# Attention and feed-forward in one kernel: query and key loads in 2.3 KB runs, keys in even/odd order, a reordered opening, and attention steps taken further ahead

## The chip, the cores and the metric

One core of a Trainium2 chip. The time is the device time of one execution in microseconds (us), as the median of several executions. The spread of one kernel's runs is under 1.5%. A ratio is the mean time of one kernel's runs over that of the kernel before's runs on the same chip in the same rounds, so it is not quite the ratio of the medians quoted beside it. A bracket is its 95% interval.

## The reference, cut to what matters

```python
# 8 batches, 8 heads, 576 tokens, head size 64; window of 32 keys on each side
scores = scale * np.matmul(q, k.transpose(0, 1, 3, 2))       # scale = 1/8
scores = np.where(np.abs(pos[:, None] - pos[None, :]) <= 32, scores, -1e9)
attn = softmax(scores);  x = (attn @ v) as 4608 tokens x 512
h = x @ w_in                                                  # 512 -> 2048
out = np.maximum(0.01 * h, h) @ w_out                         # 2048 -> 512
```

q, k and v are drawn with a standard deviation of 0.1. A score is then a sum of 64 products of about 0.01 in size, scaled by 1/8: about 0.01. Every exponential is near 1, and the attention is nearly the plain mean of the values in the window.

## The kernel before

A step of attention handles two heads ("pair") and half a batch's tokens: five score products, one exponential on ScalarE, one mask product on GpSimd, ten products for the sums `s` and the values `x`, and a reciprocal and a product on VectorE. The feed-forward tiles (`h_tile`, `o_tile`) take the result `xT` in groups of 512 tokens. q and k are loaded in blocks of 64 tokens, cast, transposed on TensorE, and copied out of PSUM into `qT` and into `kbd`, where two heads stand on the block diagonal.

```python
# loads: one packet is one token's 64 numbers (256 bytes)
nc.sync.dma_start(
    out=t[64 * s:64 * s + 64, ab].rearrange("p u c d -> p (u c) d"),
    in_=src[b, h0:h0 + 2].rearrange("u (c p) d -> p (u c) d", p=64))
# ... [cut]
def cast_v(b, u):                       # two plain casts of 64x576
    nc.gpsimd.tensor_copy(out=vbd[b % 2][0:64, u, :, 0:64], in_=vf[0:64, u])
    nc.gpsimd.tensor_copy(out=vbd[b % 2][64:128, u, :, 64:128], in_=vf[64:128, u])
# ... [cut] copies of the transposes, each writes runs of 64 elements
nc.scalar.activation(
    out=qT[b][:, :, u, 64 * c0:64 * c1].rearrange("p s (c i) -> p c s i", i=64),
    in_=tp[:, 0:n], func=AF.Copy)
for r, eng in ((0, nc.scalar), (64, nc.vector)):
    dst = kt[r:r + 64, u:NPAIR:2, c0:c1, r:r + 64].rearrange("p s c i -> p c s i")
    # ... [cut] one half copied by ScalarE, the other by VectorE
# ... [cut] the main loop: tiles of a group, with the next group's steps spread behind them
for ci, (kind, a, m) in enumerate(chunks):
    want = start + -(-(goal - start) * (ci + 1) // len(chunks))
    todo = want - state["done"]
    # ... [cut] emit the h_tiles or the o_tile of this chunk
    for _ in range(todo):
        step()
```

The softmax here doesn't subtract the row's maximum and nothing guards it: scores larger than these inputs give would overflow.

Of the kernel before, what the change touches and what calls it, by code (L numbers as in the profile page):

```python
# [16 lines left out]
def kernel(  # L17
# [15 lines left out]
    W = 32  # L33
# [8 lines left out]
    FFC = DFF // 128  # L42

# [15 lines left out]
    def load_qk(src, b, name):  # L59

        t = fload.tile([128, 2, 2, NB, D], FP32, name=name)
        for s in range(2):
            for ab in range(2):
                h0 = 4 * ab + 2 * s
                nc.sync.dma_start(  # L65
                    out=t[64 * s:64 * s + 64, ab].rearrange("p u c d -> p (u c) d"),
                    in_=src[b, h0:h0 + 2].rearrange("u (c p) d -> p (u c) d", p=64),
                )
        return t

    def load_v(b):

        t = fload.tile([128, NPAIR, NB, D], FP32, name="vf")
        for ab in range(2):
            nc.sync.dma_start(
                out=t[64 * ab:64 * ab + 64].rearrange("p u c d -> p (u c) d"),
                in_=v[b, 4 * ab:4 * ab + 4].rearrange("u (c p) d -> p (u c) d", p=64),
            )
        return t

    loaded = {}

    def load_qks(b):
        if b < B:
            loaded[b] = [load_qk(q, b, "qf"), load_qk(k, b, "kf"), None]

    def load_vs(b):
        if b < B:
            loaded[b][2] = load_v(b)

    load_qks(0)
    load_vs(0)


# [4 lines left out]

    ones_bd = const.tile([128, 128], BF16)  # L100
    nc.vector.memset(ones_bd, 0.0)
    nc.vector.memset(ones_bd[0:64, 0:64], 1.0)
    nc.vector.memset(ones_bd[64:128, 64:128], 1.0)

    kbd = [const.tile([128, NPAIR, NB, 128], BF16, name=f"kbd{i}") for i in range(2)]
    vbd = [const.tile([128, NPAIR, NB, 128], BF16, name=f"vbd{i}") for i in range(2)]
    nc.vector.memset(kbd[0], 0.0)
    nc.vector.memset(vbd[0], 0.0)
# [3 lines left out]
        [(0, 0, 128), (1, 32, 128), (2, 96, 128), (3, 160, 128), (4, 224, 64)],  # L112
        [(5, 288, 128), (6, 352, 128), (7, 416, 128), (8, 448, 128), (4, 288, 64)],
    ]
    mask = [const.tile([128, 576], BF16, name=f"mask{i}") for i in range(2)]
    for hf in range(2):
        nc.gpsimd.memset(mask[hf], 1.0)
        for lo in (0, 64):
            c0 = 0
            for blk, q0, n in WIN[hf]:  # L120
                m = mask[hf][lo:lo + 64, c0:c0 + n]

                off = q0 - 64 * blk
                nc.gpsimd.affine_select(  # L124
                    out=m, in_=m, compare_op=ALU.is_ge, fill=0.0,
                    base=off + W, channel_multiplier=-1, pattern=[[1, n]],
                )
                nc.gpsimd.affine_select(  # L128
                    out=m, in_=m, compare_op=ALU.is_ge, fill=0.0,
                    base=W - off, channel_multiplier=1, pattern=[[-1, n]],  # L130
                )
                c0 += n
# [5 lines left out]

    qb, kb, qT = {}, {}, {}

    def cast_qk(b, u):
        if b >= B:
            return
        for i, name, into in ((0, "qb", qb), (1, "kb", kb)):
            if u == 0:
                into[b] = cast.tile([128, NB, 2, 2, D], BF16, name=name)
            nc.gpsimd.tensor_copy(  # L147
                out=into[b][:, :, u], in_=loaded[b][i][:, :, u].rearrange("p a c d -> p c a d"),
            )

    def cast_v(b, u):
        if b >= B:
            return
        vf = loaded[b][2]
        nc.gpsimd.tensor_copy(out=vbd[b % 2][0:64, u, :, 0:64], in_=vf[0:64, u])
        nc.gpsimd.tensor_copy(out=vbd[b % 2][64:128, u, :, 64:128], in_=vf[64:128, u])

    def transposes(b):

        qT[b] = attn.tile([128, 2, 2, S], BF16, name="qT")  # L160
        kt = kbd[b % 2]
        for u in range(2):
            for c0, c1 in ((0, 5), (5, 9)):
                for which, src in (("q", qb[b]), ("k", kb[b])):
                    n = c1 - c0
                    tp = tps.tile([128, 5, 2, 64], BF16, name="tp")
# [6 lines left out]
                    if which == "q":  # L173
                        nc.scalar.activation(  # L174
                            out=qT[b][:, :, u, 64 * c0:64 * c1].rearrange(
                                "p s (c i) -> p c s i", i=64),
                            in_=tp[:, 0:n], func=AF.Copy,
                        )
                    else:
                        for r, eng in ((0, nc.scalar), (64, nc.vector)):  # L180

                            dst = kt[r:r + 64, u:NPAIR:2, c0:c1, r:r + 64].rearrange(
                                "p s c i -> p c s i")
                            if eng is nc.scalar:
                                nc.scalar.activation(out=dst, in_=tp[r:r + 64, 0:n], func=AF.Copy)  # L185
                            else:
                                nc.vector.tensor_copy(out=dst, in_=tp[r:r + 64, 0:n])  # L187
# [3 lines left out]

    def score(i):
        b, hf, p = i // 8, (i // 4) % 2, i % 4
        ps = scps.tile([128, 1024], FP32, name="ps")
        c0 = 0
        for blk, q0, n in WIN[hf]:
            nc.tensor.matmul(  # L197
                ps[:, c0:c0 + n], kbd[b % 2][:, p, blk, :],
                qT[b][:, p // 2, p % 2, q0:q0 + n], start=True, stop=True,
            )  # L200
            c0 += n
        e = attn.tile([128, 576], BF16, name="e")
        nc.scalar.activation(out=e, in_=ps[:, 0:576], func=AF.Exp, scale=scale)  # L203
        pr = attn.tile([128, 576], BF16, name="pr")
        nc.gpsimd.tensor_mul(pr, e, mask[hf])  # L205
        probs[i] = pr

    def weighted(i):
        b, hf, p = i // 8, (i // 4) % 2, i % 4
# [3 lines left out]
        for dst, w in ((s, None), (x, vbd[b % 2])):  # L213
            c0 = 0
            for n_, (blk, q0, n) in enumerate(WIN[hf]):
                a = q0 - HALF * hf
                nc.tensor.matmul(  # L217
                    dst[:, a:a + n], ones_bd if w is None else w[:, p, blk, :],
                    pr[:, c0:c0 + n], start=(n_ == 0), stop=(n_ == len(WIN[hf]) - 1),
                    skip_group_check=True,  # L220
                )
                c0 += n
# [8 lines left out]
    def h_tile(g, t0, n, f):  # L231
        if f == 0:
            gT[g] = moe.tile([128, FFC, 512], BF16, name="gT")
        h = mmps.tile([128, 512], FP32, name="mm")
# [5 lines left out]
        nc.scalar.activation(out=gT[g][:, f, 0:n], in_=h[:, 0:n], func=AF.Prelu, alpha=0.01)  # L240

    def o_tile(g, t0, j):
        o = mmps.tile([128, 512], FP32, name="mm")
        for f in range(FFC):
            nc.tensor.matmul(  # L245
                o, gT[g][:, f, ts(j, 128)], w_out_bf[:, f, :],
# [7 lines left out]
    NC = 2 * NPAIR * B  # L254
    t_parts = {}
    state = {"tp": 0, "done": 0}
# [9 lines left out]
    def step():  # L266
# [4 lines left out]
        step_transposes(8 * (b + 1) + -(-r * 8 // 7))  # L271
        if i + 1 < NC:
            score(i + 1)
        weighted(i)
        if r in (0, 1):
            cast_qk(b + 1, r)
        if r == 2:
            load_qks(b + 2)
        if 2 <= r < 6:
            cast_v(b + 1, r - 2)  # L280
        if r == 6:
            load_vs(b + 2)
        state["done"] += 1

    cast_qk(0, 0)
    cast_qk(0, 1)
    w_in_r = moe_w_in.rearrange("(a u d) f -> a d u f", a=2, d=D)
    for u in range(DMC):
        for a in range(2):
            nc.gpsimd.dma_start(out=w_in_bf[64 * a:64 * a + 64, u, :], in_=w_in_r[a, :, u, :])  # L290
    for u in range(NPAIR):
        cast_v(0, u)
    load_qks(1)
    load_vs(1)
    nc.vector.memset(kbd[1], 0.0)
    nc.vector.memset(vbd[1], 0.0)
    w_out_r = moe_w_out.rearrange("(c p) f -> p c f", p=128)
    for c in range(0, FFC, 4):
        nc.gpsimd.dma_start(out=w_out_bf[:, c:c + 4, :], in_=w_out_r[:, c:c + 4, :])

    step_transposes(8)
    score(0)

    groups = [(0, 256)] + [(256 + 512 * i, 512) for i in range(8)] + [(256 + 512 * 8, 256)]
    need = [4 * -(-(t0 + n) // HALF) for t0, n in groups]
    for _ in range(need[0]):
        step()

    for g, (t0, n) in enumerate(groups):
        goal = need[g + 1] if g + 1 < len(groups) else NC  # L310
        chunks = []
        per = 4 if n == 512 else 8
        for f in range(0, FFC, per):
            chunks.append(("h", f, per))
        for j in range(n // 128):
            chunks.append(("o", j, 1))
        start = state["done"]
        for ci, (kind, a, m) in enumerate(chunks):
            want = start + -(-(goal - start) * (ci + 1) // len(chunks))
            todo = want - state["done"]  # L320
            if kind == "h":
                for f in range(a, a + m):
                    h_tile(g, t0, n, f)
            else:
                o_tile(g, t0, a)
            for _ in range(todo):
                step()
        while state["done"] < goal:
            step()

# [29 lines left out]
```

## Time and profile before

| | before |
|---|---|
| time | 422.3 us (421.9 to 422.55, 3 runs) |
| TensorE busy | 80% of the span |
| first w_in product | 63.9 us |
| waits of w_in products for `xT` | 17.2 us in 8 waits |
| copies out of PSUM, 640 columns | 0.50 to 0.70 us each |

The columns are line, engine, operation, output and input with partitions x elements, count; then busy us in all, mean ns of one; then idle time before it and what ended it. From the kernel before, groups by shape:

```profile
L155 POOL CAST vbd<-vf 64x576 bf16<-64x576 f32 x32 | 21.1, 659 | 0.1
L174 ACT ACTIVATE qT<-tp 128x640 bf16<-128x640 bf16 x16 | 11.2, 701 | 53.4 <-PE tp L168 53.4
L185 ACT ACTIVATE kbd<-tp 64x640 bf16<-64x640 bf16 x16 | 11.1, 695 | 22.1 <-PE tp L168 22.1
```

### The profile page before, as it was taken

The numbers are of one execution on the slowest core, as the hardware profiler recorded it, in microseconds if no ns is written. First come the engines' busy times: TensorE is split into PE (matmuls) and PEld (weight loads), VectorE is DVE, ScalarE is ACT, GpSimd is POOL, SyncE is SP. The second block draws the span as 40 slices with busy tenths as digits, with TensorE's granted clock in tenths as the row PEclk, the third lists the DMA queues.
The fourth block names the chain that finished last, engine by engine and source line by source line (L and its number), as shares of the span: only waits on it lengthen the run. The fifth ranks groups of instructions, "written<-read, shape, count | busy, mean of one in ns | idle before, by whom it ended". The sixth has DMA issues, their size and how long they took to land.

```text
span 421.2 us, 6100 instructions
## 1 busy us (share of the span) xinstructions
PE 338.7 (80%) x2464; PEld 194.5 (46%) x2464; DVE 202.3 (48%) x204; ACT 164.5 (39%) x289; POOL 176.5 (42%) x220
## 2 busy tenths in 40 slices
PE   0231058766999799979999997999899799989996
PEld 0120046643555365545555554565455445534472
DVE  6112043866466457634445765568357735740111
ACT  1140033622752274237237525732473255116050
POOL 8992153746426443633216553654355413200000
PEclk9999999989999899989999999999899989989999
DMA  9999999445871937192450956396301100110111
GB/s 163 207 202 198 190 136 193 77 69 122 130 114 61 205 60 138 61 199 43 92 121 4 197 136 102 65 188 128 60 0 46 55 2 2 51 50 2 50 51 50
DMA packets 119835, 42.33 MB, mean 100 GB/s; under 512 B 112640, under 2 KB 114688, under 8 KB 119808
## 3 DMA queue, kind: packets, MB, share of 16 engines
q1 hardware_dynamic: 117056, 37.76, 50.7%
q0 software_dynamic: 2752, 4.20, 5.5%
q8 instruction: 19, 0.31, 0.3%
q14 instruction: 8, 0.07, 0.1%
HBM read 36.70 MB, written 9.44 MB: 110 GB/s over the span
## 4 chain that ended last, share of the span: by engine, by line
PE 73%; POOL 9%; DVE 7%; SPq 3%; issue 3%; ACT 3%; DMA 2%; POOLq 0%; DVEq 0%
PE mm L236 31%; PE mm L245 29%; DVE r L224 5%; PE s L217 3%; SPq L65 3%; PE tp L168 3%; PE x L217 3%; PE ps L197 3%; DMA kf<-in_k_dram 2%; POOL pr L205 2%; POOL mask L128 1%; POOL mask L124 1%; DVE xT L226 1%; ACT qT L174 1%; POOL w_in_bf L290 1%
## 5 line engine op out<-in xcount | busy, mean ns | idle before, releaser
L236 PE MATMUL mm<-xT,w_in_bf 128*128 128x512 bf16 (+1 forms) x640 | 142.3, 380 | 17.2 <-DVE xT L226 17.2
L224 DVE RECIPROCAL r<-s 128x288 f32<-128x288 f32 x64 | 125.2, 1957 | 58.0 <-PE s L217 56.6
L205 POOL TENSOR_TENSOR pr<-e,mask 128x576 bf16<-128x576 bf16 x64 | 81.4, 1272 | 169.2 <-ACT e L203 168.8
L245 PE MATMUL mm<-w_out_bf,gT 128*128 128x512 bf16 x576 | 130.7, 382 | 0.0
L240 ACT ACTIVATE gT<-mm 128x512 bf16<-128x512 f32 (+1 forms) x160 | 88.7, 554 | 94.0 <-PE mm L236 92.7
L236 PEld LDWEIGHTS <-w_in_bf 128*128 128x128 bf16 x640 | 64.0, 103 | 81.8 <-issue 30.0
L245 PEld LDWEIGHTS <-gT 128*128 128x128 bf16 x576 | 54.8, 99 | 62.1 <-issue 1.7
L250 DVE COPY o_sb<-mm 128x512 f32<-128x512 f32 x36 | 24.9, 691 | 70.8 <-PE mm L245 70.8
L174 ACT ACTIVATE qT<-tp 128x640 bf16<-128x640 bf16 (+1 forms) x32 | 20.7, 648 | 80.4 <-PE tp L168 80.4
L187 DVE COPY kbd<-tp 64x640 bf16<-64x640 bf16 (+1 forms) x32 | 14.8, 461 | 76.8 <-ACT kbd L185 76.7
L203 ACT ACTIVATE e<-ps 128x576 bf16<-128x576 f32 x64 | 41.2, 643 | 22.5 <-PE ps L197 22.4
L168 PE MATMUL tp<-ident,qb 128*128 128x128 bf16 x144 | 14.7, 235 | 35.7 <-POOL qb L147 31.9
L185 ACT ACTIVATE kbd<-tp 64x640 bf16<-64x640 bf16 (+1 forms) x32 | 20.5, 641 | 48.5 <-PE tp L168 48.5
L217 PE MATMUL s<-pr,ones_bd 128*128 128x128 bf16 (+1 forms) x320 | 27.7, 220 | 8.3 <-POOL pr L205 7.4
L226 DVE TENSOR_TENSOR xT<-x,r 128x288 bf16<-128x288 f32 x64 | 29.3, 458 | 6.7
L168 PEld LDWEIGHTS <-qb 128*128 128x128 bf16 x144 | 11.5, 105 | 42.0 <-POOL qb L147 32.3
L197 PE MATMUL ps<-qT,kbd 128*128 128x128 bf16 (+1 forms) x320 | 27.9, 220 | 1.2 <-ACT e L203 1.1
L217 PE MATMUL x<-pr,vbd 128*128 128x128 bf16 (+1 forms) x320 | 27.9, 220 | 0.1
L168 PE MATMUL tp<-ident,kb 128*128 128x128 bf16 x144 | 14.6, 234 | 16.0 <-ACT qT L174 8.3
L197 PEld LDWEIGHTS <-kbd 128*128 128x128 bf16 x320 | 22.6, 102 | 5.1 <-issue 2.3
L217 PEld LDWEIGHTS <-ones_bd 128*128 128x128 bf16 x320 | 20.0, 101 | 9.3 <-DVE r L224 5.0
L147 POOL CAST qb<-qf 128x1152 bf16<-128x1152 f32 x16 | 18.3, 1143 | 12.2 <-DMA qf<-in_q_dram 12.1
(25 smaller groups left out, 123.2 us busy)
## 6 DMA issues: line engine op xcount, KB each, us to landing
qf<-in_q_dram SPq DMA_DIRECT2D x32, 288.0 KB, 5.3
kf<-in_k_dram SPq DMA_DIRECT2D x32, 288.0 KB, 6.1
vf<-in_v_dram SPq DMA_DIRECT2D x16, 576.0 KB, 7.5
out_dram<-o_sb SPq DMA_DIRECT2D x36, 256.0 KB, 2.1
w_in_bf<-in_moe_w_in_dram POOLq DMA_DIRECT2D x8, 256.0 KB, 9.0
w_out_bf<-in_moe_w_out_dram POOLq DMA_DIRECT2D x4, 512.0 KB, 13.1
```

What stands on the lines that cost most here:

```text
L168: nc.tensor.transpose(tp[:, c - c0].rearrange("p s i -> p (s i)"), src[:, c, u].rearrange("p a d -> p (a d)"), ident,)
L174: nc.scalar.activation(out=qT[b][:, :, u, 64 * c0:64 * c1].rearrange("p s (c i) -> p c s i", i=64), in_=tp[:, 0:n], func=AF.Copy,)
L197: nc.tensor.matmul(ps[:, c0:c0 + n], kbd[b % 2][:, p, blk, :], qT[b][:, p // 2, p % 2, q0:q0 + n], start=True, stop=True,)
L203: nc.scalar.activation(out=e, in_=ps[:, 0:576], func=AF.Exp, scale=scale)
L205: nc.gpsimd.tensor_mul(pr, e, mask[hf])
L217: nc.tensor.matmul(dst[:, a:a + n], ones_bd if w is None else w[:, p, blk, :], pr[:, c0:c0 + n], start=(n_ == 0), stop=(n_ == len(WIN[hf]) ...
L224: nc.vector.reciprocal(r, s)
L226: nc.vector.tensor_mul(xT[:, p, t0:t0 + HALF], x, r)
L236: nc.tensor.matmul(h[:, 0:n], w_in_bf[:, c, ts(f, 128)], xT[:, c, ds(t0, n)], start=(c == 0), stop=(c == DMC - 1),)
L240: nc.scalar.activation(out=gT[g][:, f, 0:n], in_=h[:, 0:n], func=AF.Prelu, alpha=0.01)
L245: nc.tensor.matmul(o, gT[g][:, f, ts(j, 128)], w_out_bf[:, f, :], start=(f == 0), stop=(f == FFC - 1),)
L250: nc.vector.tensor_copy(out=o_sb, in_=o)
```

## The change

The intent: fewer and larger load packets; only 544 instead of 576 columns of scores in a step, with the sums in two wide products instead of five; an opening in which the loads, casts and weights come in the order in which they are needed; and attention steps done earlier than the group that needs them. The price of the long load runs is the order of the data. A partition now holds nine neighbouring tokens (9 x 256 bytes = 2304), so a transposed block holds every ninth token. The copies out of PSUM put them back in order by writing every 9th element of `qT`. For `kbd`, where even and odd keys also alternate, they write every 18th.

```diff
-                    in_=src[b, h0:h0 + 2].rearrange("u (c p) d -> p (u c) d", p=64),
+                        in_=src[b, h0:h0 + 2].rearrange("u (p c) d -> p u (c d)", c=NB)[:, us],
...
-        nc.gpsimd.tensor_copy(out=vbd[b % 2][0:64, u, :, 0:64], in_=vf[0:64, u])
-        nc.gpsimd.tensor_copy(out=vbd[b % 2][64:128, u, :, 64:128], in_=vf[64:128, u])
+        for a in range(2):
+            nc.gpsimd.tensor_scalar_mul(
+                vbd[b % 2][:, u, :, 64 * a:64 * a + 64], vf[b][:, u], par[:, a:a + 1],
+            )
...
-                            out=qT[b][:, :, u, 64 * c0:64 * c1].rearrange(
-                                "p s (c i) -> p c s i", i=64),
+                            out=qT[b][:, :, u].rearrange("p s (i c) -> p c s i", c=NB)[:, c0:c1],
                             in_=tp[:, 0:n], func=AF.Copy,
...
-                            dst = kt[r:r + 64, u:NPAIR:2, c0:c1, r:r + 64].rearrange(
-                                "p s c i -> p c s i")
+                            dst = kbd[b % 2][r, u:NPAIR:2].rearrange(
+                                "p s (i c a) -> p a c s i", c=NB, a=2)[:, a, c0:c1]
...
+        nc.tensor.matmul(s, ones_bd, pr[:, 0:HALF], start=True, stop=False, skip_group_check=True)
+        nc.tensor.matmul(
+            s[:, ODD[hf]:ODD[hf] + NCOL - HALF], ones_bd, pr[:, HALF:NCOL],
+            start=False, stop=True, skip_group_check=True,
+        )
...
+    LEAD = 2
+    base = state["done"]
+    span = len(chunks) - 10
+    for ci, (_, kind, t0, n, a, m) in enumerate(chunks):
+        ahead = chunks[min(ci + LEAD, len(chunks) - 1)][0]
+        goal = max(ahead, base + -(-(NC - base) * (ci + 1) // span))
+        while state["done"] < min(goal, NC):
             step()
```

Cut: the masks by even and odd keys, the loads and casts of the first batch in halves, the weights in quarters of their columns, the second batch's load behind the last weight piece, and the order of the first three groups.

## The prediction

> **What bounds the kernel now.** I read the page's slices first, then the chain of waits in order of time, then the groups by shape, then TensorE's timeline. The slices split the run in two:
>
> ```profile
> PE   0231058766999799979999997999899799989996
> DMA  9999999445871937192450956396301100110111
> ...
> DMA packets 119835, 42.33 MB, mean 100 GB/s; under 512 B 112640, under 2 KB 114688, under 8 KB 119808
> ```
>
> A digit is 10.5 us. For the first 66 us TensorE is mostly idle and DMA is full, nearly all of it in packets under 512 bytes; after some 104 us TensorE is at 9 with a dip about every 40 us. The chain says what each half waits for:
>
> ```profile
> 35.88 7.30 SPq L65
> 43.23 4.80 SPq L65
> 48.08 6.66 DMA kf<-in_k_dram
> ...
> 181.58 1.97 DVE r L224
> 183.64 0.47 DVE xT L226
> 184.16 4.65 PE mm L236 x13
> 188.81 0.28 PE tp L168 x5
> 189.84 6.91 PE mm L236 x32
> ```
>
> In the opening it is the second batch's key load, stuck behind weights and short packets. Later it is, once per group of 512 tokens, the reciprocal of the last attention step: the group's first w_in product needs it at once. TensorE waits 2.29 us there, and then 13 products take 4.65 us, 358 ns each, where 32 take 6.91 us, 216 ns each. So such a wait costs 2.3 us and often 1.7 us of half clock. The chain has five such slow stretches after 104 us (143, 184, 296, 337 and 374 us).
>
> The rows by shape that I use:
>
> ```profile
> L224 DVE RECIPROCAL r<-s 128x288 f32<-128x288 f32 x64 | 125.2, 1957 | 58.0 <-PE s L217 56.6
> ...
> L226 DVE TENSOR_TENSOR xT<-x,r 128x288 bf16<-128x288 f32 x64 | 29.3, 458 | 6.7
> ...
> L187 DVE COPY kbd<-tp 64x640 bf16<-64x640 bf16 x16 | 7.9, 495 | 59.2 <-ACT kbd L185 59.2
> L187 DVE COPY kbd<-tp 64x512 bf16<-64x512 bf16 x16 | 6.8, 428 | 17.6 <-ACT kbd L185 17.5
> ```
>
> An attention step keeps VectorE 1.96 + 0.46 us, about 2.55 with gaps, but TensorE only 0.76: in the timeline five score products start 0.25 us before the next five. Where two steps stand back to back, TensorE's timeline shows the price:
>
> ```profile
> 79.97 0.42 PE L217 MATMUL s<-pr,ones_bd 128*128 128x128 bf16 x5
> 80.23 0.42 PE L217 MATMUL x<-pr,vbd 128*128 128x128 bf16 x5
> 80.62 0.38 PE L168 MATMUL tp<-ident,kb 128*128 128x128 bf16 x4
> 81.17 0.41 PE L197 MATMUL ps<-qT,kbd 128*128 128x128 bf16 x5 [0.16 <-ACT e L203]
> 82.58 0.41 PE L217 MATMUL s<-pr,ones_bd 128*128 128x128 bf16 x5 [1.00 <-POOL pr L205]
> 83.00 0.41 PE L217 MATMUL x<-pr,vbd 128*128 128x128 bf16 x5
> 83.25 3.62 PE L245 MATMUL mm<-w_out_bf,gT 128*128 128x512 bf16 x16
> ```
>
> The second s product comes 2.61 us after the first. The two steps began at 79.50, so they took 3.75 us for some 2.0 us of TensorE work. The s accumulator has one buffer, so the next s waits for the reciprocal.
>
> As a check, sum TensorE from 104.27 us: 68 chunks (16 products of 512 columns, 3.45 us) 234.8, 52 steps at 0.76 39.5, 44 transpose parts at 0.25 11, less 0.7 done, 284.6. Add seven waits of 2.29 (16.0), five slow stretches (8.5), six waits of 0.79 where a step has two transpose parts (4.7) and 4.0 from the last product to the end: 422, measured 421.2. I use the same sum for the changed kernel.
>
> **What the Trainium skill says.** "DMA: Bandwidth & Descriptors", Specifications, puts the least transfer for line rate at 512 bytes. The trace agrees: its packets of 256 bytes took 26.8 ns in the mean, those of 2 KB 93 ns, eight times the bytes for 3.5 times the time. "TensorE: Matmul & The Clock Gate", Part 1, says that idle TensorE drops to half clock and returns after a busy window of about 3.4 us; the 4.65 us stretch agrees. The same page, Back-to-back issue gap, gives N/2.4 + 2.5 ns per product: 216 ns at 512 columns, as above. "Advanced Engine Details and Errata", 2x-1p Requirements, asks unit step of 16-bit data for two elements per cycle. The key copies of before slope (495-428)/128 = 0.52 ns an element, two per cycle[...]; the changed ones write every 18th element, so I estimate 0.83 and 0.70 us.
>
> **The change, part by part.**
>
> Loads. A batch's q and k are 9216 packets of 256 bytes before, 15.4 us of 16 engines at 26.8 ns; now 1024 of 2304 bytes, about 6.5 us at some 100 ns (estimate from the 2 KB packet). The second batch waits for the last w_out piece, so the weights run alone.
>
> Opening (estimates). q and k of half a batch land near 6 and 9 us. VectorE's cast, four transposes and key copies give score 0 near 12 us, before 27.5. GpSimd then casts v (8 of about 0.7 us) and issues 12 weight loads at 0.6 to 0.8 us, so its second mask product ends only near 29.6 us. Steps 1 to 5 follow at VectorE's 2.7 us; the first w_in product starts near 41 (before 63.9). Both first 256-token groups run: 64 products each at 110 ns warm, two steps, about 4 us of cold clock, to 59.7; two w_out tiles to 66.6 us. Then the second batch's eight transposes stand with nothing beside them, through one PSUM buffer: before took 12.9 us cold for them (15.8 to 28.75), now with slower key copies 12 to 13, so score 8 comes near 78.5. Step 8's exp and mask, two w_out tiles (the first partly cold) and steps 9 to 12, held by reciprocals, end near 100.4 us.
>
> Steady part from there: 64 chunks at 3.45 are 221. A step is 0.71 us now (544 columns three times; s in two products, 122.5 + 109 ns): 51 are 36.2. 43 transpose parts 10.8, five two-part waits 4, tail 4. With 100.4 that is 376.4 us without stalls. The narrower steps themselves save only about 3 us over the run.
>
> Stalls. The eight waits at group starts go, since the steps a group needs are done two chunks earlier. But the new loop does not spread them. Counting its goals: before chunk 2 and chunk 10 six steps stand together, before 18 and 26 two, before 34, 42 and 50 three. TensorE's order of instructions in the changed kernel confirms the first two runs. Six steps take 1.0 + 5 x 2.55 + two key copies of 0.83 = 15.4 us, for 5.8 us of TensorE work: 9.6 lost. Three with transposes: 1.0 + 2 x 2.55 + 1.1 (transpose, copies, then reciprocal) = 7.2, for 2.9: 4.3 lost; without, 4.0. Two: 1.75, as measured. Sum 2 x 9.6 + 2 x 1.75 + 2 x 4.3 + 4.0 = 35.3. Half-clock stretches after seven such runs, about 1.2 each from five of seven at 1.7: 8.5. Together 44 us, against 29 of the same kinds before.
>
> Sum: 376.4 + 44 = 420. In terms of before: the opening gives some 20 us of lead at equal work, the steps 3, and the bunched steps take back about 15 more than the group waits did.
>
> **Rivals.** First, the bunches cost little: if half-clock hides inside the VectorE wait, key copies keep their speed and the opening comes 5 us earlier, the stalls are about 34 and the end near 404. For it: every serial sum of waits tends to count overlaps twice. Against: s has one buffer and the reciprocal is unchanged. Second, the opening is worse: GpSimd's scaled v casts may be slower than its plain ones (0.66 us for 64x576), and it issues the weights before it masks; each extra 0.3 us over eight casts is 2.4 us, and a late batch 1 lengthens the hole near 67 us. That gives 430. Third, DMA is the bound and its relief is worth all the opening's idle time, 35 us or more, with group waits gone as intended and bunches absorbed: about 380 to 390. The full DMA slices speak for it; against it, DMA is already far from full after 70 us and TensorE's own work alone is some 310.
>
> **Range and chances.** I set 417 us, a little under the sum because its estimates are serial. Errors of about 5 us in the opening and 10 in the stalls make 398 to 431 the range for 8 in 10. Two per cent under 422.3 is 413.9, close below my value: faster 0.43, within 0.47, slower 0.10.
>
> **What would show it.** Right: first w_in product near 41 us; a hole of about 10 us at 66 to 79 with transposes on the chain; no wait of w_in on xT; in its place s waiting for the reciprocal or the mask, in two runs of six steps of about 15 us near 110 and 160 us; key copies near 0.83 us; q and k packets near 100 ns. Wrong: if the six-step runs take under 12 us, if the weights land after 50 us, or if TensorE's slices are at 9 from 45 us on, the sum fails at that term.

## The result, and the profile after

The changed kernel takes 548.59 us (547.14 to 548.82, 4 runs) against 422.1 us (419.2 to 422.55) of the kernel before: ratio 1.3008 [1.2945, 1.3071]. It is slower, and far outside the predicted range. The result is right.

The slices of the changed kernel, each 13.7 us, and its chain by engine:

```profile
PE   1203891136573699439978786968496859979996
PEclk9999996559595599658979897989698978998999
...
PE 50%; DVE 18%; ACT 17%; issue 7%; POOL 6%; SPq 2%; DMA 1%; DVEq 0%; POOLq 0%
PE mm L263 21%; PE mm L254 20%; ACT kbd L195 9%; DVE kbd L197 9%; DVE r L242 7%; ACT qT L184 5%; PE tp L178 3%; PE x L236 2%; POOL vbd L162 2%; POOL pr L220 2%; SPq L72 2%; PE s L228 2%; ACT e L216 1%; PE s L229 1%; POOL w_in_bf L312 1%
```

TensorE is no longer at 9 from the middle on. It keeps falling to 3 to 6, with the granted clock at 5 or 6 in many of the earlier dips. In the kernel before, TensorE was 73% of the chain, ScalarE 3% and VectorE 7%. Now ScalarE and VectorE have 35%, and 23 points of it are three lines: the copies of keys and queries out of PSUM. The rows by shape say why:

```profile
L162 POOL TENSOR_SCALAR vbd<-vf,par 128x576 bf16<-128x576 f32 x64 | 109.6, 1729 | 3.1 <-DMA vf<-in_v_dram 3.1
L216 ACT ACTIVATE e<-ps 128x544 bf16<-128x544 f32 x64 | 53.8, 840 | 51.8 <-PE ps L210 51.6
L197 DVE COPY kbd<-tp 64x640 bf16<-64x640 bf16 x18 | 52.3, 2907 | 79.5 <-ACT kbd L195 74.2 <-PE tp L178 5.2
L184 ACT ACTIVATE qT<-tp 128x640 bf16<-128x640 bf16 x16 | 47.8, 2987 | 39.1 <-PE tp L178 39.1
...
L195 ACT ACTIVATE kbd<-tp 64x640 bf16<-64x640 bf16 x14 | 40.7, 2905 | 16.8 <-PE tp L178 16.8
```

Compare with the rows before: the same copy of 640 columns takes 2.9 to 3.0 us in place of 0.50 to 0.70, on both engines. The v cast takes 1.73 us in place of 0.66. The prediction had 0.83 us for the key copies, no change for the query copies, and 0.7 for the v casts.

The chain in order of time (start, us, what) shows what these copies do where they stand alone, in the second batch's transposes:

```profile
83.50 0.29 PE tp L178 x5
...
83.81 2.99 ACT qT L184
...
86.84 0.45 PE tp L178 x5
...
87.32 2.91 ACT kbd L195
...
90.25 2.91 DVE kbd L197
```

There is one PSUM buffer for transposes, and VectorE's half of a key copy starts when ScalarE's half ends. So all copies of a batch stand in line. With the sizes 640 and 512 taken twice each, before: queries 2 x (0.70 + 0.60) = 2.6 us, keys 2 x (0.70 + 0.59 + 0.50 + 0.43) = 4.4 us, 7 us a batch. After: 2 x (2.99 + 2.45) = 10.9 and 2 x (2.91 + 2.36 + 2.91 + 2.35) = 21.1, 32 us a batch. Seven batches follow the first; 25 us more for each is 175 us, and what of it does not hide beside tiles is the loss. What TensorE waits for (us in all, number of waits, longest), changed kernel:

```profile
PE tp L178 <- DVE kbd L197: 47.7, 17, 5.9
PE s L228 <- DVE r L242: 37.6, 28, 3.3
PE tp L178 <- ACT qT L184: 32.3, 11, 3.3
```

The first and third line are waits for copies, 80 us together. The second is for the most part the bunched steps that the prediction had, each sum waiting for the reciprocal before it; with packed copies and plain casts (e5 below) 23.6 us of it are left.

The loads did what they were to do, only less. Packets fell from 119835 to 56062, and the share of all 16 DMA engines that the load and store queue took fell from 50.7% of 421 us to 30.0% of 547 us. In the trace's packet records a packet of 2304 bytes took 168 ns in the mean, not the 100 ns of my estimate, which is 13.7 bytes per ns against 11.4 of the 256-byte packets (22.5 ns) beside them.

### The profile page after: what moved, and what is told of

Its sections match the earlier page's. It is cut to its first block, busy times and chain, and to the rows that moved or that the text cites. A ratio compares the mean times of both kernels' runs of the same rounds, so it can differ in the third digit from the quotient of the medians.

```text
span 547.1 us, 5823 instructions
## 1 busy us (share of the span) xinstructions
PE 375.4 (69%) x2336; PEld 211.2 (39%) x2336; DVE 279.1 (51%) x213; ACT 282.1 (52%) x301; POOL 229.6 (42%) x179
## 2 busy tenths in 40 slices
DMA packets 56062, 42.31 MB, mean 77 GB/s; under 512 B 39140, under 2 KB 43236, under 8 KB 56036
## 4 chain that ended last, share of the span: by engine, by line
PE 50%; DVE 18%; ACT 17%; issue 7%; POOL 6%; SPq 2%; DMA 1%; DVEq 0%; POOLq 0%
PE mm L263 21%; PE mm L254 20%; ACT kbd L195 9%; DVE kbd L197 9%; DVE r L242 7%; ACT qT L184 5%; PE tp L178 3%; PE x L236 2%; POOL vbd L162 2%; POOL pr L220 2%; SPq L72 2%; PE s L228 2%; ACT e L216 1%; PE s L229 1%; POOL w_in_bf L312 1%
## 5 line engine op out<-in xcount | busy, mean ns | idle before, releaser
L220 POOL TENSOR_TENSOR pr<-e,mask 128x544 bf16<-128x544 bf16 x64 | 77.7, 1216 | 237.7 <-ACT e L216 237.6
L197 DVE COPY kbd<-tp 64x640 bf16<-64x640 bf16 (+1 forms) x36 | 94.6, 2628 | 110.8 <-ACT kbd L195 105.5
L184 ACT ACTIVATE qT<-tp 128x640 bf16<-128x640 bf16 (+1 forms) x32 | 86.5, 2719 | 71.8 <-PE tp L178 71.8
L162 POOL TENSOR_SCALAR vbd<-vf,par 128x576 bf16<-128x576 f32 x64 | 109.6, 1729 | 3.1 <-DMA vf<-in_v_dram 3.1
L195 ACT ACTIVATE kbd<-tp 64x640 bf16<-64x640 bf16 (+1 forms) x28 | 73.7, 2631 | 19.8 <-PE tp L178 19.6
L216 ACT ACTIVATE e<-ps 128x544 bf16<-128x544 f32 x64 | 53.8, 840 | 51.8 <-PE ps L210 51.6
L228 PE MATMUL s<-pr,ones_bd 128*128 128x288 bf16 x64 | 22.5, 351 | 54.8 <-DVE r L242 37.6
L210 PE MATMUL ps<-qT,kbd 128*128 128x128 bf16 (+2 forms) x320 | 32.5, 245 | 19.5 <-DVE kbd L197 15.9
L178 PE MATMUL tp<-ident,kb 128*128 128x128 bf16 x144 | 17.2, 264 | 34.6 <-ACT qT L184 32.3
L236 PE MATMUL x<-pr,vbd 128*128 128x128 bf16 (+2 forms) x320 | 32.9, 247 | 1.7 <-DVE xT L244 1.7
L236 PEld LDWEIGHTS <-vbd 128*128 128x128 bf16 x320 | 26.3, 117 | 12.0 <-issue 7.1
```

The costliest lines, as they stand in the source:

```text
L162: nc.gpsimd.tensor_scalar_mul(vbd[b % 2][:, u, :, 64 * a:64 * a + 64], vf[b][:, u], par[:, a:a + 1],)
L178: nc.tensor.transpose(tp[:, c - c0].rearrange("p s i -> p (s i)"), src[:, c, u].rearrange("p a d -> p (a d)"), ident,)
L184: nc.scalar.activation(out=qT[b][:, :, u].rearrange("p s (i c) -> p c s i", c=NB)[:, c0:c1], in_=tp[:, 0:n], func=AF.Copy,)
L195: nc.scalar.activation(out=dst, in_=tp[r, 0:n], func=AF.Copy)
L197: nc.vector.tensor_copy(out=dst, in_=tp[r, 0:n])
L216: nc.scalar.activation(out=e, in_=ps[:, 512 - HALF:512 - HALF + NCOL], func=AF.Exp, scale=scale,)
```

## The experiments

The theory after the first look: the scattered writes of the copies make the loss, and the scaled v casts a small part. The rivals: the v casts on GpSimd make most of it, as they hold up weights and masks in the opening; or the new order of steps does.

**e1: the changed kernel, copies write packed runs of 64.** The data end in the wrong order. The comparison with the reference did not notice, since the attention is nearly a plain mean; this run says nothing about correctness.

```diff
-   out=qT[b][:, :, u].rearrange("p s (i c) -> p c s i", c=NB)[:, c0:c1],
+   out=qT[b][:, :, u].rearrange("p s (c i) -> p c s i", c=NB)[:, c0:c1],
-       "p s (i c a) -> p a c s i", c=NB, a=2)[:, a, c0:c1]
+       "p s (c a i) -> p a c s i", c=NB, a=2)[:, a, c0:c1]
```

> The changed kernel with one thing undone: the copies of the transposed q and k write runs of 64 neighbouring elements again instead of every 9th or 18th (the result is wrong on purpose, the instructions and their number are the same). Theory A, scattered writes are the cause: the copies fall from 2.4 to 3.0 us to 0.4 to 0.7 us and the time from 548.6 to 420 to 440 us. Theory B, the bunched steps and the new opening are the cause: the copies fall but the time stays above 500 us. Theory C, GpSimd's scaled v casts (1.73 us) are: the time stays above 520 us.

438.34 us, ratio 1.0425 [1.0368, 1.0482]. That is theory A: 110 of the 126 us lost go with the order of the writes alone. The copies are back at 701, 697 and 493 ns.

**e2: the changed kernel, q and k loaded in blocks of 64 tokens again.** The result is right. The queries are then packed, and the keys go to every second element.

```diff
-   in_=src[b, h0:h0 + 2].rearrange("u (p c) d -> p u (c d)", c=NB)[:, us],
+   in_=src[b, h0:h0 + 2][us].rearrange("u (c p) d -> p (u c) d", p=64),
    (cut: the writes of the copies, changed to match)
```

> The changed kernel with q and k loaded in blocks of 64 tokens again (runs of 256 bytes), so that qT is written packed and the keys with a step of 2 elements; right result, all else as changed. Theory A: 425 to 445 us, within 10 us of the run with packed writes, q copies near 0.7 us, key copies at most 1 us; the 256-byte loads cost little, since they lie beside other work. Theory B or C: above 500 us. A fourth theory, that the 2.3 KB runs are worth much: 20 us or more slower than the run with packed writes.

447.95 us, ratio 1.0641 [1.0598, 1.0684], 3 us above the range of theory A and far below that of the others. The key copies take 874 ns on VectorE: my 0.83 us was right for a step of two elements, and only for that. It is about 10 us slower than e1. That is what the long runs would be worth in this schedule if their order were free, together with 0.3 to 0.4 us on each VectorE key copy and 0.15 to 0.19 on each of ScalarE's.

**e3: the kernel before, with nothing but its copies' writes scattered to every 9th and 18th element.** The order is wrong, and again it was not noticed.

```diff
-   out=qT[b][:, :, u, 64 * c0:64 * c1].rearrange("p s (c i) -> p c s i", i=64),
+   out=qT[b][:, :, u].rearrange("p s (i c) -> p c s i", c=NB)[:, c0:c1],
-   dst = kt[r:r + 64, u:NPAIR:2, c0:c1, r:r + 64].rearrange("p s c i -> p c s i")
+   dst = kt[r:r + 64, u:NPAIR:2].rearrange("p s n k -> p s (n k)").rearrange(
+       "p s (i c a) -> p a c s i", c=NB, a=2)[:, r // 64, c0:c1]
```

> The kernel before with one thing added: its copies of the transposed q and k write every 9th or 18th element (wrong result on purpose). Theory A: copies of 2.4 to 3.0 us here too, and 480 to 540 us. Theory B or C, which put the cost into the new schedule or the v casts: within 440 us, the longer copies being hidden beside the w_in and w_out products.

557.14 us, ratio 1.3231 [1.3172, 1.329]; theory A had given 480 to 540. The row of the VectorE copies, 495 ns each in the kernel before:

```profile
L186 DVE COPY kbd<-tp 64x640 bf16<-64x640 bf16 x16 | 46.5, 2905 | 101.9 <-ACT kbd L184 101.9
```

The scattered writes alone cost the kernel before 135 us, with neither loads, casts nor schedule changed. The rivals cannot explain this run.

**e4: the changed kernel with plain v casts** (wrong values, relative error 0.93). **e5: e1 and e4 together** (likewise).

```diff
-   nc.gpsimd.tensor_scalar_mul(
-       vbd[b % 2][:, u, :, 64 * a:64 * a + 64], vf[b][:, u], par[:, a:a + 1],
+   nc.gpsimd.tensor_copy(
+       out=vbd[b % 2][:, u, :, 64 * a:64 * a + 64], in_=vf[b][:, u],
```

> The changed kernel with GpSimd's scaled v casts (multiplied by a per-partition factor) replaced by plain casts of the same shape (wrong result on purpose). Theory C: each falls from 1.73 to about 0.66 us and the time drops by 40 us or more. Theory A: only the opening gains, 5 to 10 us, as the mask product of step 1 comes some 8 us earlier and part of that is lost to the weights' landing: 538 to 545 us.

> Both costs taken away at once: packed writes of the copies and plain v casts, the rest as changed (wrong result on purpose). If the scattered writes and the scaled casts are all that the prediction missed, the time is that of its sum, 412 to 424 us. If the two hide each other, the plain casts gain more here (15 to 26 us against packed writes alone, 438.3) than the 9 us that they gained beside scattered writes. If some third cost is left, it stays above 430 us.

e4: 539.55 us, ratio 1.2808 [1.2752, 1.2864]. e5: 423.05 us, ratio 1.0038 [0.9976, 1.0101]. The four kernels make a table of both causes:

| us | plain v casts | scaled v casts |
|---|---|---|
| packed writes | 423.05 (e5) | 438.34 (e1) |
| scattered writes | 539.55 (e4) | 548.59 (changed) |

Scattered writes cost 539.55 - 423.05 = 116.5 us, the scaled casts 15.3 alone and 9.0 beside the scattered writes. The parts do not add up exactly (131.8 against 125.5): where both costs stand, some of one hides behind the other.

e5 is the changed kernel without the two costs, and it lands 3 us from the prediction's sum of 420. So close a fit is partly luck: its key copies on VectorE take 0.49 us where I had assumed 0.83. Two of its rows and three places of TensorE's timeline (start, us, what) show how far the rest of the working held:

```profile
L162 POOL CAST vbd<-vf 128x576 bf16<-128x576 f32 x64 | 40.5, 670 | 3.1 <-DMA vf<-in_v_dram 3.1
...
L197 DVE COPY kbd<-tp 64x640 bf16<-64x640 bf16 x18 | 8.9, 493 | 30.2 <-ACT kbd L195 24.4 <-PE tp L178 5.8
```

```profile
42.21 3.35 PE L254 MATMUL mm<-xT,w_in_bf 128*128 128x256 bf16 x16
...
98.00 4.53 PE L254 MATMUL mm<-xT,w_in_bf 128*128 128x256 bf16 x32
...
112.76 0.30 PE L228 MATMUL s<-pr,ones_bd 128*128 128x288 bf16 x1 [1.81 <-DVE r L242]
```

The first w_in product comes at 42.2 us (predicted 41), the transposes' hole begins at 66.3 in the same timeline (predicted 66), the steady part at 98.0 (predicted 100.4). The last line is from the first run of six steps. There the sum waits for the reciprocal of the step before. The whole run, from its first transpose to the next w_out product, takes from 106.9 to 123.7 us: 16.8 in place of the predicted 15.4, though its key copies are shorter than assumed. The second run (154.8 to 171.6 us) takes 16.8 as well.

**p1: what a scattered write costs.** The kernel before, with a row of test copies of 64x640 from PSUM at its end, three of each; one look only, 569.41 us with the probe, state unknown. Only the durations of the copies are used.

```diff
+    for _ in range(3):  # bf16 step 4; likewise 1, 2, 3, 6, 8, 9, 16, 18, fp32, and on ScalarE
+        nc.vector.tensor_copy(out=xf[0:64, 0:2560:4], in_=sl)
```

> The kernel before with a row of copies of 64x640 added after its last product, from the same PSUM tile to SBUF, on VectorE and then on ScalarE, three of each: bf16 written with a step of 1, 2, 3, 4, 6, 8, 9, 16 and 18 elements; the same writes with the loop order turned, so that 5 neighbours are written one after the other; and fp32 with a step of 1, 2, 4 and 9. If the cost is that each write falls on another line of 16 bytes: fast up to a step of 4 elements in bf16 (two writes to a line), slow from 8 on, turned order fast, fp32 fast at step 2 and slow from 4 on. If any 2-byte write without its neighbour costs: slow from step 2 on, fp32 never slow. If only large steps cost: slow at 16 and 18 alone. Packed: 0.50 us on VectorE and 0.70 us on ScalarE; step 18: 2.9 us on both.

Groups by shape of the probe; the lines are steps 1 (L343), 2 (L345), 4 (L349) and 8 (L353) on VectorE:

```profile
L353 DVE COPY xT<-tp 64x640 bf16<-64x640 bf16 x3 | 8.9, 2976 | 0.1
...
L349 DVE COPY xT<-tp 64x640 bf16<-64x640 bf16 x3 | 4.7, 1564 | 0.1
...
L345 DVE COPY xT<-tp 64x640 bf16<-64x640 bf16 x3 | 2.6, 858 | 0.1
...
L343 DVE COPY xT<-tp 64x640 bf16<-64x640 bf16 x3 | 1.4, 479 | 0.1
```

ScalarE shows the same from step 3 on (1225, 1577, 2990, 2897 ns at steps 3, 4, 8, 18; 697 at step 1). The time grows with the step up to 8 elements, which is 16 bytes, and then stays (2882 ns at step 18). From step 3 to step 8 it fits 0.15 us plus 4.4 ns for each 16-byte line that the copy visits: at step 4 two elements share a line, 320 lines, 1.56 us; at step 8 640 lines, 2.97 us. This agrees in kind with the Trainium skill, "Advanced Engine Details and Errata", SBUF Cachelines: lines of 16 bytes, and a penalty for a different line at each access. The page gives no size for the penalty. It also says that two hits on a line are needed to absorb the latency; here two were not enough, for at a step of 4 each line takes two writes and the copy still took 1.56 us against 0.48 packed. None of the three expectations fits as a whole. Against the one of lines, bf16 was slow before a step of 8, and a write of float32 rose only from 0.82 us (steps 1 and 2) to 1.27 and 1.28 us (steps 4 and 9). So the 4.4 ns hold for bf16 alone; why float32 pays less was not tested.

**f1: the changed kernel, copies walk the output in order.** If the cost is per line visited, the copy should finish a line before it goes on. The loops of both sides are turned: the four or five neighbours that go beside each other are written one after the other, and PSUM is read with a step instead. The result is right.

```diff
-   out=qT[b][:, :, u].rearrange("p s (i c) -> p c s i", c=NB)[:, c0:c1],
-   in_=tp[:, 0:n], func=AF.Copy,
+   out=qT[b][:, :, u].rearrange("p s (i c) -> p s i c", c=NB)[:, :, :, c0:c1],
+   in_=tp[:, 0:n].rearrange("p c s i -> p s i c"), func=AF.Copy,
    (the key copies likewise)
```

> The changed kernel with the loop order of the copies turned: the same elements go to the same places, but neighbours (5 or 4 tokens) are written one after the other and the step lies in the read from PSUM; right result. If the cost is per 16-byte line visited, as the row of test copies says: key copies of 5 blocks 1.27 us, q copies about 0.8 us, and 440 to 452 us, most of the 110 us back without giving up the 2.3 KB loads. If it is the set of places that costs, whatever the order: no gain, about 548 us.

457.28 us, ratio 1.0847 [1.0779, 1.0915], 5 us above the range: the order of the loops gives back 91 us. The copies of 640 columns take 763 ns (queries) and 1295 to 1298 ns (keys).

**f2: f1, and v loaded into a tile of zeros with the gaps in place,** so that one plain cast of 1152 columns takes the place of two scaled ones. The first batch's v loads moved behind the clearing of that tile. The result is right.

```diff
-   nc.gpsimd.tensor_scalar_mul(vbd[b % 2][:, u, :, 64 * a:64 * a + 64], vf[b][:, u], par[:, a:a + 1])
+   nc.gpsimd.tensor_copy(out=vbd[b % 2][:, u], in_=vz[:, u])
```

> The turned order, and v loaded into a tile with zeros in the other head's half, so that one plain GpSimd cast of 1152 columns (about 1.15 us) takes the place of two scaled ones (3.45 us); right result. Expected 416 to 430 us: GpSimd's v work falls from 109 to about 37 us and leaves the chain. If GpSimd was not what bounded after the first repair: no gain against the turned order alone.

446.14 us, ratio 1.058 [1.0503, 1.0657]; 11 us less than f1, but 16 above the range. The two scaled casts of 1.73 us became one of 1.15. TensorE's waits for a mask product of GpSimd fell from 21.8 to 10.3 us, while those for a reciprocal rose from 24.3 to 27.1; f3 takes these up.

**f3: f2, with the steps spread evenly between the starts of two groups,** one chunk ahead of need, instead of the changed loop's goals. The result is right.

```diff
-    LEAD = 2
-    goal = max(ahead, base + -(-(NC - base) * (ci + 1) // span))
+    LEAD = 1
+    (goals laid evenly from the chunk of one need to the chunk of the next)
```

> As the run with padded v, with the attention steps spread evenly between the group starts (one or two between chunks, done one chunk ahead) in place of runs of six and three; right result. Theory of the prediction, that the bunched steps cost some 44 us of waits and half clock where spread ones would cost about 10: 385 to 402 us, faster than the kernel before. If the bunches cost little: within 8 us of the padded v run.

406.71 us, ratio 0.965 [0.9591, 0.9708], 5 us above the range, but faster than the kernel before. The same line of TensorE's waits, f2 and then f3:

```profile
PE s L227 <- DVE r L241: 27.1, 21, 2.5
```

```profile
PE s L227 <- DVE r L241: 8.3, 9, 1.6
```

39.4 us for the spreading, of which 18.8 are these waits. Most of the rest goes with the clock: the mean granted clock of the profiled execution rises from 0.88 to 0.93, and TensorE's busy time falls from 355.1 to 337.3 us for the same work. The bunched steps were the largest cost that the prediction saw (44 us, waits and half clock together), and they were real.

**g1: f3 with block loads. g2: the kernel before with one move,** its steps ahead of each chunk's tiles instead of behind. Both results are right.

```diff
 g2
+            for _ in range(todo):
+                step()
             if kind == "h":
                 ...
-            for _ in range(todo):
-                step()
```

> The kernel with spread steps (406.7 us), its query and key loads alone put back to 256-byte block loads, which lets the query copies read and write packed again (about 0.70 us each, estimated from 701 ns) and the key copies write every second element (about 0.87 us, estimated from 874 ns) in place of about 1.29. Theory: the loads in runs of 2304 bytes are worth less than the dearer copies and their slower landing cost, since the DMA engines are not what ends the waits of the steady part: 398 to 406 us. Rival: the loads in runs are what brought the gain of the opening: 412 us or more. Result should be right.

> The kernel before with one move alone: the steps of attention that belong to a chunk are emitted ahead of that chunk's tile work instead of behind it. Theory: it is the schedule, not the loads, the key order or the casts, that the fast version lives by: the eight waits of about 2.3 us at group starts and the stretches at a lower TensorE clock go, 394 to 407 us. Rival: the opening and the loads bound the kernel before and the move only shifts the waits: 415 to 425 us. Result should be right.

g1: 394.41 us, ratio 0.9368 [0.9323, 0.9413], better than both theories had it. g2: 396.62 us, ratio 0.9418 [0.9375, 0.9462]. g1 against f3 says that the 2304-byte loads together with the turned copies that they need cost 12 us. g2 says that moving two lines of the kernel before has nearly all of the gain of the best version found, and without any of the change. The w_in row of the kernel before, and then of g2:

```profile
L236 PE MATMUL mm<-xT,w_in_bf 128*128 128x512 bf16 (+1 forms) x640 | 142.3, 380 | 17.2 <-DVE xT L226 17.2
```

```profile
L236 PE MATMUL mm<-xT,w_in_bf 128*128 128x512 bf16 (+1 forms) x640 | 130.6, 360 | 0.0
```

The 17.2 us of waits are gone, and 11.7 us of slow products with them. My reading of the kernel before had 16.0 and 8.5 for the two, 24.5 together; g2 gained 25.0. Since the two rows add up to 28.9, a fit within 0.5 us is partly luck.

**g3: g1 with the second batch's transposes woven between products.** In g1's timeline the eight transposes still stand alone from 69.2 to 81.7 us. Two w_out tiles were put between them, and the four steps after them stand together.

```diff
-    step_transposes(16)
+    for j in range(2):
+        o_tile(256, j, lambda: step_transposes(state["tp"] + 1))   # one part after each 4 products
     score(8)
...
-    for j in range(2):
-        step()
-        o_tile(256, j)
-    step()
-    step()
+    for _ in range(4):
+        step()
```

> The kernel with spread steps and block loads (394.4 us), with one move in the opening: the second batch's eight transposes stand between the quarters of the two w_out tiles of the second 256 tokens, in place of by themselves, and the four attention steps after them stand together. Theory: what is left of the opening's lead is lost in the transposes' hole (69.2 to 81.5 us with nothing beside it), so some 8 of its waits hide under 7 us of products, while the steps after it were bounded by the reciprocal anyway: 386 to 391 us. Rival: the second batch's key load (cast at 67.7 us) and the reciprocals form a chain that does not shorten, so the products only change places: 393 to 396 us. Result should be right.

406.24 us, ratio 0.962 [0.9603, 0.9637]: slower than g1 by 12 us, and outside what either theory gave. TensorE's timeline shows a third thing:

```profile
96.18 0.71 PE L176 MATMUL tp<-ident,qb 128*128 128x128 bf16 x5 [11.13 <-POOL qb L156]
103.68 0.71 PE L176 MATMUL tp<-ident,kb 128*128 128x128 bf16 x5 [6.78 <-POOL kb L156]
```

The hole was filled, but the next step then waited for the third batch's q and k. The cause is my edit: the loads of that batch come from SyncE's queue, which takes its entries in order. Behind the four output stores of the first 512 tokens they were issued from 84.5 us on; in g1, where two of the stores came later, from 70.6.

**g4: g3 with these loads ahead of the two stores. g5: g4 with the 2304-byte loads and the turned copies.** Both results are right. They were run to settle where the opening's lead of some 20 us had gone.

```diff
 g4
+    new_qk(2); load_qk(2, slice(0, 2)); load_v(2, slice(0, 4))
     for j in range(2):
         o_tile(256, j, lambda: step_transposes(state["tp"] + 1))
     score(8)
-    new_qk(2); load_qk(2, slice(0, 2)); load_v(2, slice(0, 4))
```

> The woven opening (406.2 us) with the third batch's loads issued ahead of the two output stores that stood before them. Theory: the 11.1 and 6.8 us of waiting for the third batch's queries and keys come from the place of the loads in SyncE's in-order queue (84.5 us in place of 70.6), so they go for the most part, and the hole of transposes stays filled: 386 to 391 us. Rival: the loads themselves bound the opening, so that the third batch's keys still come late and the time stays at 393 us or more. Result should be right.

> The same with the 2304-byte loads and the copies that walk their output in order. If the opening is bounded by loads once its transposes are hidden, the long runs bring the second and third batch earlier and make up for the dearer copies: within 4 us of the version with block loads or faster. If the copies are what counts, it is 8 to 15 us slower than that version, as before (406.7 against 394.4). Result should be right.

g4: 393.37 us, ratio 0.9302 [0.9256, 0.9348]. g5: 403.28 us, ratio 0.9532 [0.9488, 0.9576]. The place in the queue was the whole of g3's loss, 12.9 us. But with it mended, g4 is only 1 us faster than g1, which ran in another set of runs, and the intervals of the two ratios overlap: the rival was right about the time. TensorE's waits in g4:

```profile
PE s L227 <- DVE r L241: 8.2, 9, 1.1
PE tp L176 <- POOL kb L156: 7.5, 3, 3.4
```

The steady part begins at 105.1 us in g4 and at 106.1 in g1. Filling the hole only moved the waits: the third batch's first key cast waits for its load until 89.7 us, and after it four steps stand bare, each sum behind a reciprocal, at a granted clock of 0.50 between 90 and 100 us. And g5 is 10 us slower than g4: even where loads end a wait of the opening, the long runs do not pay for their copies.

## Why the prediction was wrong

**The step that failed** is the cost of the copies in "What the Trainium skill says": "the changed ones write every 18th element, so I estimate 0.83 and 0.70 us". It took the loss of two elements per cycle as the only price of a step. The runs show 2.91 and 2.35 us for these copies. The query copies on ScalarE were not in the sum at all, and went from 0.70 and 0.60 to 2.99 and 2.45 us. The mis-sized term cost 116.5 us (e4 against e5), and e3 gets a like loss (135 us) from the kernel before with that edit alone. The section that I cited was true for the mode, which e2 confirms at step 2 (874 ns). The section on cachelines on the same page was the one that mattered.

**A second term, right in kind and small in size:** the v casts, "8 of about 0.7 us". The scaled ones took 1.73 us. The second rival named this danger, at "0.3 us" each; it was 1.0, worth 15.3 us beside packed copies and 9.0 beside scattered ones.

**A third term:** 2304-byte packets at "some 100 ns" took 168. e5 reached the predicted milestones within 3 us all the same, so it moved the sum little.

**What was right:** the reading of the kernel before (g2 gained 25.0 us for the 24.5 read), the opening's times, the hole of transposes, the bunches of six steps (16.8 us each for 15.4), and that the new loop gives back in bunches what it gains at the group starts. With packed copies and plain casts the kernel takes 423.05 us. No rival had dearer copies. One comparison in the prediction is uneven: its "29 of the same kinds before" contains 4.7 us of two-part waits, and its 44 does not. Like for like it is 44 against 24.5, so the bunches were to take back about 20, not 15; the sum of 420 does not rest on this.

**Where the expected gain went:** without the copies and casts, the opening's lead and the group waits were given back to bunched steps (e5, no gain); spreading them was worth 39.4 us (f3 against f2). The opening's lead is real: the first w_in product comes at 42 us in e5, against 63.9. To follow it, count at equal work. The changed order starts its steady part with 64 tiles of 3.45 us left, four fewer (13.8 us) than the kernel before has at 104.3 us. So e5, at 98.0 us, is some 19 us ahead, as predicted. g1, at 106.1 us, is still about 12 us ahead of the kernel before, and 8 ahead of g2, which starts its last 68 tiles at 100.6 us. But g1 ends only 2 us before g2. By 150 us most of these 8 are gone: from its start TensorE is busy for 38.1 of 43.9 us at a clock of 0.93 in g1, and for 48.6 of 49.4 us at 1.00 in g2. Up to 106 us, the timelines of g1 and g4 show the second and third batch loaded, transposed and stepped through one after the other, with little else for TensorE to do between. What a version would gain that shortens that chain was not tried, and what takes the rest after 106 us was not separated.

## What to carry to other kernels

Where a change reorders data, look for the instruction that pays for the order, and price its access pattern on the side that it writes as well as on the side that it reads, in lines visited and not in elements. If an order must be turned, let the copy walk its output and read with the step. And before rebuilding loads, layouts and schedule at once, try the smallest edit that removes the wait on the chain: here moving one loop ahead of its tiles gave 6%. When a load moves, look at what stands ahead of it in its queue.

## What the Trainium skill lacked or had wrong

- "Advanced Engine Details and Errata", SBUF Cachelines: right in kind, but without a size. A bf16 copy from PSUM to SBUF fits 0.15 us plus 4.4 ns for each 16-byte line visited, from a step of 3 elements on, on VectorE and ScalarE alike (64x640: 0.48 us packed on VectorE, 2.98 us at a step of 8 elements). The two hits on a line that it asks for were not enough: 1.56 us at a step of 4 elements. It says that the tolerance of a stride depends on the type, but not how: float32 writes took 1.28 us at a step of 9. Turning the loop of the copy, so that neighbours on a line follow each other, repaired most of it (2.99 to 0.76 us for the query copies).
- "GPSIMD Engine Reference", 4.1 Engine selection, calls one-input operations roughly line-rate on GpSimd. The plain cast of 128x576 took 0.67 us, 1.16 ns an element, but the product with a factor per partition of the same size, if that counts as one input, took 1.73 us, 2.6 times as long.
- A trap in reading the trace, on no page that I found: the exponential of 128x544 took 0.84 us in the mean in the changed kernel and 0.62 us in e1, which differs only in the writes of the copies. ScalarE's records show why. The 44 exponentials that come directly behind a scattered copy have 0.92 to 0.97 us, but each starts about 0.5 us before the record of the copy ends; the other 20 have 0.62 us. From the end of the copy's record to its own end it takes 0.45 us, no more than the 0.51 to 0.55 in e1 behind a packed copy. So the longer record is overlap with the copy's end, and not a dearer exponential.
